# Ending the second batch of a fused top-k attention and MLP kernel the way the first one ends, and re-pacing the layer products around it

## The chip, the core and the metric

One core of a Trainium2 chip runs the whole program. The metric is the device time of one execution in microseconds (us). The kernel before takes 1860.23 us (median of three runs, 1859.75 to 1863.38). The engines are TensorE (PE; PEld is its weight load), VectorE (DVE), ScalarE (ACT), GpSimd (POOL) and SyncE (SP), which issues most of the transfers. Each engine works through its own list of instructions in the order in which the kernel emits them; they meet through semaphores.

## The reference: what is computed

```python
# q, k, v: (8 batches, 8 heads, 576 rows, 64)
scores = matmul(q, k^T) / 8                     # 576 x 576 for each head
kth    = the 32nd largest of each row
scores = where(scores >= kth, scores, -1e9)     # keep the top 32 of a row
attn   = softmax(scores);  o = matmul(attn, v)
x      = o, heads side by side                  # (8, 576, 512)
# then, for each batch, a low-rank mixer over the rows and a two-layer MLP
h = x^T @ U @ V                                 # U: 576 x 32, V: 32 x 576
u = x + h^T
out = u + relu(u @ w1) @ w2                     # w1: 512 x 2048, w2: 2048 x 512
```

Everything is in float32 at the end; the weights U, V, w1, w2 arrive as float64 and the kernel makes float32 of them itself while the first batches run.

The MLP of a batch needs all four head pairs of that batch, since the mixer and both layers work on all 512 columns. So the layer products of batch b can only be computed once the attention of batch b is done. The kernel computes them beside the attention of batch b + 1, and those of the last batch stand alone at the end.

## The kernel before

The work is cut into 160 steps, counted from 0. A step is one block of rows of one head pair: `g, t = divmod(n, 5)`, blocks t = 0 to 3 have 128 rows for each of the two heads (two row chunks of 576 scores), and block t = 4 has the last 64 rows of both heads in one chunk. A batch is 4 pairs, 20 steps. The top 32 of a row are found on VectorE, eight at a time, with four MAX8 and three MATCH_REPLACE8. The weighing of a chunk (exponential on ScalarE, then everything under the 32nd largest set to zero) is spread over three engines:

```python
def front(g, t):
    ...
    for c in order:                              # VectorE: the first eight of each chunk
        nc.vector.max(ms[c], curs[c])            # L320
    yield
    pooled = n == 2 and (g, t) != (NPAIR - 1, NT - 1)
    for i in range(1, TOPK // 8):
        if i == 1:
            nc.scalar.mul(nmax[:, 0:n], first[:, 0:n, 0], -SCALE)
            for c in range(1 if pooled else n):
                weigh(chunks[c], Es[c], nmax[:, c : c + 1])        # L300, ScalarE: exp
        ...                                      # match_replace (L330) and max (L334) by chunk
        yield
    if pooled:                                   # second chunk: mask on GpSimd, exp afterwards
        nc.gpsimd.tensor_scalar(Es[1], chunks[1], ms[1][:, 7:8], NEG, ALU.is_lt, ALU.mult)  # L337
        nc.gpsimd.tensor_tensor(chunks[1], chunks[1], Es[1], ALU.add)                       # L338
    for c in range(1 if pooled else n):          # otherwise: exp first, mask on VectorE
        nc.vector.scalar_tensor_tensor(out=Es[c], in0=chunks[c], scalar=ms[c][:, 7:8],      # L340
                                       in1=Es[c], op0=ALU.is_ge, op1=ALU.mult, accum_out=sums[c])
    ...
    yield
    if pooled:
        weigh(chunks[1], Es[1], nmax[:, 1:2], sums[1])
    yield
```

What follows for a block: `turns` transposes its weights on TensorE and copies them back on ScalarE (three parts, two for t = 4; each part ends in a `yield`), `values` multiplies them with v. When all five blocks of a pair are done, `mixed` transposes the pair's result, scales it by the reciprocals of the row sums (`inverse`, on VectorE; the scaling on GpSimd) and adds the low-rank mixer. After the fourth pair of a batch it puts `mlp(b)`, the layer products, on the list `fillers`:

```python
def inverse(g, lo, hi):
    den = dens[g][:, lo:hi]
    nc.vector.tensor_scalar_add(den, den, 1e-9)  # L378
    nc.vector.reciprocal(den, den)               # L379

def values(g, t):
    ...
    if t == NT:
        inverse(g, 2 * NT if g == NPAIR - 1 else 0, 2 * NT + 1)
    ...

def mixed(g, wait):
    ...                                          # transposes, copy, scaling on GpSimd (L429)
    for _ in range(wait):
        yield
    ...                                          # pT (L435), Tb, up (L447, L449), uT (L457)
    if gi == NPAIR - 1:
        fillers.append(mlp(b))
```

`mlp` yields after each matmul of the first layer (L472) and the second (L491). After each group of four row blocks' columns its result is added to u on GpSimd (L507, on VectorE in the last batch) and turned back by transposes (L519) some matmuls later; the last group is turned back right at the end. One `fill()` places as many layer matmuls as its share allows, and advances the mixing of a pair by one piece:

```python
SLOTS, SHORT, EARLY = 8, 0.65, 0.91
share = MLP_WORK / (NPAIR * SLOTS * (NT + SHORT))

def fill(k=1):
    nonlocal due
    for _ in range(k):
        if mixing and next(mixing[0], True):
            mixing.pop(0)
        due += share * (SHORT if t == NT else 1) * (EARLY if n <= 2 * ALONE + 2 else 1)
        while due > 0:
            if not fillers:
                due = 0.0
                break
            done = next(fillers[0], None)
            ...                                  # due -= done
```

`ALONE` is 20, the number of steps in a batch. The main loop has three forms of a step: one for the first batch (no layer products yet), one for steps 19 and 20, the end of the first batch, and one for all later ones (cut here to the order of its calls):

```python
for n in range(STEPS + 2):
    ...
    if n >= ALONE - 1 and n <= ALONE:            # steps 19 and 20
        list(turning)
        if n < ALONE:
            scores(*divmod(n + 1, CH))
        list(turns(*divmod(n - 1, CH)))
        if n < ALONE:
            values(*divmod(n - 2, CH))
            next(here)                           # step 19's exponential is emitted here
        values(*divmod(n - 1, CH))
        if n < ALONE:
            inverse(g, 0, 2 * NT)
            next(here)
            mixing.append(mixed(g, 1))
            fill(); next(here); next(here)
            continue
        fill(); scores(*divmod(n + 1, CH)); next(here)
        while mixing:
            fill()
        ...
        continue
    if n < ALONE:
        ...                                      # first batch
        continue
    # later batches: values lag by two steps, the mixing of a pair by one more
    fill(); next(turning, None); fill(); next(turning, None); fill(); next(ready, None); fill()
    if n - 2 >= ALONE:
        values(*divmod(n - 2, CH))
    if n + 1 < STEPS:
        scores(*divmod(n + 1, CH))
    next(here, None)                             # the exponential
    ...
    if n - 2 >= ALONE and (n - 2) % CH == NT:
        mixing.append(mixed((n - 2) // CH, 4))
    fill(); next(here, None); fill()
    if n <= STEPS:
        turning = turns(*divmod(n - 1, CH))
    next(turning, None); fill(); next(here, None); next(last, None); ...; fill()
while mixing or fillers:
    fill()
```

Of the kernel before, what the change touches and what calls it, by code (L numbers as in the profile page):

```python
# [24 lines left out]
def kernel(  # L25
# [35 lines left out]
    NT, TAIL = 4, 64  # L61
# [3 lines left out]
    NPAIR = H // 2  # L65
    NP = B * NPAIR
    SCALE = 1.0 / float(D) ** 0.5
    NV = 3
    HT = 10
    PE, ACT = mybir.EngineType.PE, mybir.EngineType.Activation  # L70
# [231 lines left out]
    def front(g, t):  # L302

        if t == 0:
            dens[g] = small.tile([P, 2 * NT + 1], F32, tag="den", name="den", bufs=3)
        chunks, den = S2s.pop((g, t)), dens[g]
        n = len(chunks)
        E2 = attn.tile([P, 2 * S], F32, tag="E", name="E", bufs=3)  # L310
        Es = [E2[:, c * S : (c + 1) * S] for c in range(n)]
        sums = [den[:, 2 * t + c : 2 * t + c + 1] for c in range(n)]
        probs[g, t] = E2
        curs, ms = list(chunks), [None] * n
        first = small.tile([P, 2, 8], F32, tag="first", name="first", bufs=3)
        nmax = small.tile([P, 2], F32, tag="nmax", name="nmax", bufs=4)
        order = (1, 0) if n == 2 else (0,)
        for c in order:
            ms[c] = first[:, c]
            nc.vector.max(ms[c], curs[c])  # L320
        yield
        pooled = n == 2 and (g, t) != (NPAIR - 1, NT - 1)
        for i in range(1, TOPK // 8):
            if i == 1:
                nc.scalar.mul(nmax[:, 0:n], first[:, 0:n, 0], -SCALE)
                for c in range(1 if pooled else n):
                    weigh(chunks[c], Es[c], nmax[:, c : c + 1])
            for c in order:
                nxt = attn.tile([P, S], F32, tag="rr", name="rr", bufs=3)
                nc.vector.match_replace(nxt, ms[c], curs[c], NEG)  # L330
                curs[c] = nxt
            for c in order:
                ms[c] = small.tile([P, 8], F32, tag="m8", name="m8", bufs=8)
# [6 lines that stand above are left out]
            nc.vector.scalar_tensor_tensor(  # L340
                out=Es[c],
                in0=chunks[c],
                scalar=ms[c][:, 7:8],
                in1=Es[c],
                op0=ALU.is_ge,
                op1=ALU.mult,
                accum_out=sums[c],
            )
        if t == NT:
            del qkTs[g]  # L350
# [4 lines that stand above are left out]
# [21 lines left out]
# [7 lines that stand above are left out]
        PT = PTs.pop((g, t))  # L383
        va, vd, vt = (a[g % NV] for a in (vas, vds, vts))
        O = ps_t.tile([P, P], F32, tag="tp", name="O")
        if t == NT:
            den, x = dens[g], xs[g % 2]
            inverse(g, 2 * NT if g == NPAIR - 1 else 0, 2 * NT + 1)
            for j in range(NT + 1):
                nc.tensor.matmul(  # L390
                    O,
                    lhsT=PT[:, j],
                    rhs=va[:, :, j, :] if j < NT else vt,
                    start=(j == 0),
                    stop=(j == NT),
                )
            for h in range(2):
                nc.scalar.mul(x[half(h), NT, half(h)], O[half(h), half(h)], den[half(h), 2 * NT :])
            return
        nc.tensor.matmul(O, lhsT=vd, rhs=PT[:, 2 * NT], start=True, stop=False)  # L400
        for j in range(NT):
            for h in range(2):
                nc.tensor.matmul(  # L403
                    O[half(h)],
                    lhsT=va[:, h, j, :],
                    rhs=PT[:, NT * h + j],
                    start=False,
                    stop=(j == NT - 1),
                )
        if t == 0:  # L410
            XTs[g] = attn.tile([P, MAIN], F32, tag="XT", name="XT")
        nc.scalar.copy(XTs[g][:, cols(t)], O)  # L412
# [124 lines left out]
    CH = NT + 1  # L537
    STEPS = NP * CH
    ALONE = NPAIR * CH


    SLOTS, SHORT, EARLY = 8, 0.65, 0.91
    share = MLP_WORK / (NPAIR * SLOTS * (NT + SHORT))
    fillers, mixing, due = [], [], 0.0

    def fill(k=1):

        nonlocal due
        for _ in range(k):
            if mixing and next(mixing[0], True):  # L550
                mixing.pop(0)
            due += share * (SHORT if t == NT else 1) * (EARLY if n <= 2 * ALONE + 2 else 1)
            while due > 0:
                if not fillers:
                    due = 0.0
                    break
                done = next(fillers[0], None)
                if done is None:
                    fillers.pop(0)
                else:  # L560
                    due -= done

    load(0)
    next_params(1)
    t = 0
# [5 lines left out]
    for n in range(STEPS + 2):  # L571
        g, t = divmod(n, CH)
        if n < STEPS:
            if t == 0 and g + 1 < NP:
                load(g + 1)
            if t == 1 and g + 1 < NP:
                ready = prep(g + 1)
            fronts[n] = front(g, t)
            next(fronts[n])
        here, last = fronts.get(n, iter(())), fronts.pop(n - 1, iter(()))  # L580
        if n >= ALONE - 1 and n <= ALONE:

            list(turning)
            if n < ALONE:
                scores(*divmod(n + 1, CH))
            list(turns(*divmod(n - 1, CH)))
            if n < ALONE:
                values(*divmod(n - 2, CH))
                next(here)
            values(*divmod(n - 1, CH))  # L590
            if n < ALONE:
                inverse(g, 0, 2 * NT)
                next(here)
                mixing.append(mixed(g, 1))
# [9 lines that stand above are left out]
            next_params(1)  # L604
            fill()
            next(last, None)
# [7 lines that stand above are left out]
            next(turning, None)  # L614
            next(turning, None)
            scores(*divmod(n + 1, CH))
            fill()
            if n >= 1:
                turning = turns(*divmod(n - 1, CH))
            if n >= 2:  # L620
                values(*divmod(n - 2, CH))
            next(here)
            next_params(1)
            next(turning, None)
            fill()
            next(last, None)
            next(ready, None)
            next(here)
            fill()
            if n >= 2 and (n - 2) % CH == NT:  # L630
                mixing.append(mixed((n - 2) // CH, 3))
            next(here)
            if t == 1:
                next_params(1)
# [4 lines that stand above are left out]
        next(turning, None)  # L639
        fill()  # L640
        next(turning, None)
        fill()
        next(ready, None)
        fill()
        if n - 2 >= ALONE:
            values(*divmod(n - 2, CH))
        if n + 1 < STEPS:
            scores(*divmod(n + 1, CH))
        next(here, None)
        next_params(1)  # L650
        if n - 2 >= ALONE and (n - 2) % CH == NT:
            mixing.append(mixed((n - 2) // CH, 4))
        fill()
        next(here, None)
# [3 lines that stand above are left out]
        next(turning, None)  # L658
        fill()
        next(here, None)  # L660
        next(last, None)
        if t in (1, 3):
            next_params(1)
        next(here, None)
        fill()
# [33 lines left out]
```

## Time and profile before

| | before |
|---|---|
| time | 1860.23 us |
| TensorE busy | 1750.6 us (94%) |
| its weight loads busy | 1324.0 us (71%) |
| VectorE busy | 1617.2 us (87%) |
| ScalarE busy | 1008.1 us (54%) |
| GpSimd busy | 635.7 us (34%) |
| layer matmuls, both layers (L472, L491) | 557.9 + 562.2 us, 2048 each |
| MAX8 and MATCH_REPLACE8 (L320, L330, L334) | 205.4 + 639.6 + 614.8 us |

The trace counts two matmuls for each float32 matmul of the program that is not a transpose. The span of the profiled execution, 1861.6 us, falls into three parts: the first batch's attention alone (to about 224 us), seven batches in which attention and the layer products of the batch before run side by side (to about 1706 us), and the last batch's products alone (155 us). A share over the whole span mixes these; where the batches matter, the busy times have to be taken stretch by stretch. A busy TensorE in these profiles is modelled from pipelined matmuls and is not a TensorE at its peak.

### The profile page before, as it was taken

To read this page: it belongs to the slowest core of one execution; us is meant where nothing else is said; L and a number is where in the kernel's file an instruction comes from. 1 tells how busy PE (TensorE), PEld (TensorE's weight loads), DVE (VectorE), ACT (ScalarE), POOL (GpSimd) and SP (SyncE) were. 2 spreads that over 40 slices of the span, in tenths; PEclk is the share of its full clock that TensorE was granted. 3 is DMA by queue.
4 is the path that set the end of the run, shared out by engine and by line. 5 is a ranking of instruction groups with operands and counts; after the bars stand their busy time and mean duration, and the time that the engine had idled before them with its cause. 6 is when DMAs were issued, how large, how long until landed. Compare 5 with 4: busy or idle time off the path is not lost.

```text
span 1861.6 us, 29241 instructions
## 1 busy us (share of the span) xinstructions
PE 1750.6 (94%) x10528; PEld 1324.0 (71%) x10528; DVE 1617.2 (87%) x3316; ACT 1008.1 (54%) x2466; POOL 635.7 (34%) x432
## 2 busy tenths in 40 slices
PE   4565789999999999999999999999999999999999
PEld 3443556787777877788777877788777877788677
DVE  7999999999999999999999999999999999996000
ACT  4666677555655555555555555555555555554111
POOL 4556466433333332323233332332323332322000
PEclk7677799999999999999999999999999999999999
DMA  3222222101000010110001010101001010000000
GB/s 98 76 72 75 63 81 81 28 23 32 15 21 22 23 29 21 30 25 24 23 13 31 21 32 20 28 22 27 14 24 27 25 30 21 10 8 7 6 14 12
DMA packets 127296, 58.23 MB, mean 31 GB/s; under 512 B 89904, under 2 KB 124976, under 8 KB 127152
## 3 DMA queue, kind: packets, MB, share of 16 engines
q1 hardware_dynamic: 126096, 56.10, 11.3%
q8 instruction: 84, 1.38, 0.3%
q14 instruction: 60, 0.49, 0.1%
q10 hardware_dynamic: 1056, 0.26, 0.1%
HBM read 46.89 MB, written 9.44 MB: 30 GB/s over the span
## 4 chain that ended last, share of the span: by engine, by line
PE 84%; DVE 10%; ACT 4%; issue 1%; POOL 1%; DMA 0%; POOLq 0%; SPq 0%; DVEq 0%; ACTq 0%
PE mm L472 27%; PE mm L491 26%; PE sc L274 9%; PE O L403 6%; PE tp L367 6%; DVE rr L330 4%; DVE m L334 3%; PE O L390 2%; PE up L447 2%; PE O L400 1%; DVE first L320 1%; PE tp L254 1%; PE tp L519 1%; PE up L449 1%; PE tp L372 1%
## 5 line engine op out<-in xcount | busy, mean ns | idle before, releaser
L334 DVE MAX8 m<-rr 128x8 f32<-128x576 f32 x864 | 614.8, 749 | 5.5
L491 PE MATMUL mm<-hT,w 128*128 128x256 f32 (+1 forms) x2048 | 562.2, 410 | 0.0
L472 PE MATMUL mm<-uT,w 128*128 128x256 f32 (+1 forms) x2048 | 557.9, 411 | 1.5 <-ACT hT L484 1.5
L337 POOL TENSOR_SCALAR E<-Ssb,m 128x576 f32<-128x576 f32 x127 | 285.2, 2246 | 650.7 <-DVE m L334 512.7
L472 PEld LDWEIGHTS mm<-uT,w 128*128 128x128 f32 x2048 | 363.3, 190 | 108.6 <-issue 27.6
L491 PEld LDWEIGHTS mm<-hT,w 128*128 128x128 f32 x2048 | 360.5, 190 | 97.7 <-issue 22.5
L330 DVE MATCH_REPLACE8 rr<-m,rr 128x576 f32<-128x576 f32 x576 | 427.8, 743 | 0.0
L367 PE MATMUL tp<-ident,E 128*128 128x128 f32 x1152 | 184.7, 285 | 53.8 <-ACT E L300 38.7
L368 ACT COPY PT<-tp 128x512 f32<-128x512 f32 x288 | 168.4, 585 | 114.9 <-PE tp L367 113.0
L300 ACT ACTIVATE E<-Ssb,nmax 128x576 f32<-128x576 f32 x288 | 223.8, 778 | 5.9 <-POOL Ssb L338 0.7
L367 PEld LDWEIGHTS tp<-ident,E 128*128 128x128 f32 x1152 | 144.9, 147 | 106.9 <-ACT E L300 50.7
L274 PE MATMUL sc<-qkT 64*128 64x288 f32 (+1 forms) x1280 | 212.5, 454 | 0.3 <-ACT Ssb L293 0.3
L330 DVE MATCH_REPLACE8 rr<-first,Ssb 128x576 f32<-128x576 f32 x288 | 211.8, 742 | 0.0
L320 DVE MAX8 first<-Ssb 128x8 f32<-128x576 f32 x288 | 205.4, 750 | 0.9 <-ACT Ssb L295 0.9
L340 DVE SCALAR_TENSOR_TENSOR E<-Ssb,m,E 128x576 f32<-128x576 f32 x161 | 137.8, 856 | 65.6 <-ACT E L300 48.2
L338 POOL TENSOR_TENSOR Ssb<-Ssb,E 128x576 f32<-128x576 f32 x127 | 178.9, 1408 | 10.6
L484 ACT ACTIVATE hT<-mm 128x320 f32<-128x320 f32 (+1 forms) x256 | 104.4, 408 | 119.8 <-PE mm L472 119.0
L412 ACT COPY XT<-O 128x128 f32<-128x128 f32 x128 | 34.0, 266 | 215.1 <-PE O L403 215.1
L403 PE MATMUL O<-PT,va 128*64 128x128 f32 x2048 | 147.7, 289 | 0.0
L274 PEld LDWEIGHTS sc<-qkT 64*128 64x128 f32 (+1 forms) x1280 | 110.2, 187 | 51.7 <-issue 25.4
L504 DVE TENSOR_TENSOR oT<-uT,mm 128x320 f32<-128x320 f32 (+1 forms) x8 | 3.6, 455 | 146.6 <-PE mm L491 146.6
L403 PEld LDWEIGHTS O<-PT,va 128*64 128x64 f32 x2048 | 116.0, 143 | 16.8 <-issue 2.9
(73 smaller groups left out, 1484.3 us busy)
## 6 DMA issues: line engine op xcount, KB each, us to landing
raw<-in_moe_w_ch_dram SPq DMA_DIRECT2D x32, 512.0 KB, 3.7
va<-in_v_dram SPq DMA_DIRECT2D x64, 128.0 KB, 2.5
out_dram<-ob SPq DMA_DIRECT2D x64, 128.0 KB, 1.9
ld_q<-in_q_dram SPq DMA_DIRECT2D x63, 128.0 KB, 2.8
ld_k<-in_k_dram SPq DMA_DIRECT2D x63, 128.0 KB, 2.8
ld_ends<-in_q_dram SPq DMA_DIRECT2D x32, 32.0 KB, 2.2
ld_ends<-in_k_dram SPq DMA_DIRECT2D x32, 32.0 KB, 2.2
vd<-in_v_dram SPq DMA_DIRECT2D x64, 16.0 KB, 2.0
```

Source lines behind the costliest of these rows:

```text
L274: nc.tensor.matmul(sc[slice(0, n) if t < NT else half(h), h, 0:HALF], lhsT=qkT[half(h), 0, cols(t)], rhs=qkT[half(h), 1, i * HALF : (i + 1 ...
L300: nc.scalar.activation(E, chunk, AF.Exp, bias=nmax, scale=SCALE, accum_out=total)
L320: nc.vector.max(ms[c], curs[c])
L330: nc.vector.match_replace(nxt, ms[c], curs[c], NEG)
L334: nc.vector.max(ms[c], curs[c])
L337: nc.gpsimd.tensor_scalar(Es[1], chunks[1], ms[1][:, 7:8], NEG, ALU.is_lt, ALU.mult)
L338: nc.gpsimd.tensor_tensor(chunks[1], chunks[1], Es[1], ALU.add)
L367: nc.tensor.transpose(tp[:, j, :], E2[:, a : a + P], ident)
L368: nc.scalar.copy(PT[:, NT * h : NT * h + NT], tp)
L403: nc.tensor.matmul(O[half(h)], lhsT=va[:, h, j, :], rhs=PT[:, NT * h + j], start=False, stop=(j == NT - 1),)
L472: nc.tensor.matmul(ph[:, 0:w], lhsT=w1[:, cc, f * P : (f + 1) * P], rhs=uT[:, cc, lo:hi], start=(cc == 0), stop=(cc == NC - 1),)
L491: nc.tensor.matmul(po[:, 0:w], lhsT=w2[:, f, c * P : (c + 1) * P], rhs=hTs[f][:, 0:w], start=(f == 0), stop=(f == NF - 1),)
```

## The change

The second batch gets the ending of the first. In its last step (step 39) the exponential of the short block, the last transposes and both remaining value products are emitted at once rather than trailing into steps 41 and 42, and the mixing of its last pair is done in step 40; the second batch's products can then begin right behind it. Unlike at the first batch, there are products of the batch before to be placed beside this, so the ending calls `fill` between its parts; `fill(False)` places products without advancing the mixing. Step 38's second chunk, too, is weighed without GpSimd, and the reciprocals of the pair's sums are taken in two parts. For the first batch's products to be finished by then, they go faster beside the second batch (pace 1.02 in place of 0.91), and those beside the third go slower (0.91 in place of 1), so that they last until the next ones are ready.

```diff
+    WAITED = (NPAIR - 1, 2 * NPAIR - 1)
...
-        pooled = n == 2 and (g, t) != (NPAIR - 1, NT - 1)
+        pooled = n == 2 and not (g in WAITED and t == NT - 1)
...
-            inverse(g, 2 * NT if g == NPAIR - 1 else 0, 2 * NT + 1)
+            inverse(g, 2 * NT if g in WAITED else 0, 2 * NT + 1)
...
-    SLOTS, SHORT, EARLY = 8, 0.65, 0.91
+    SLOTS, SHORT, PACE = 8, 0.65, {1: 1.02, 2: 0.91}
...
-    def fill(k=1):
+    def fill(mix=True):
         nonlocal due
-        for _ in range(k):
-            if mixing and next(mixing[0], True):
-                mixing.pop(0)
-            due += share * (SHORT if t == NT else 1) * (EARLY if n <= 2 * ALONE + 2 else 1)
+        if mix and mixing and next(mixing[0], True):
+            mixing.pop(0)
+        due += share * (SHORT if t == NT else 1) * PACE.get((n - 1) // ALONE, 1)
...
-        if n >= ALONE - 1 and n <= ALONE:
+        if (n + 1) // CH - 1 in WAITED and t in (NT, 0):
             list(turning)
-            if n < ALONE:
+            fill(t != 0)
+            if t:
                 scores(*divmod(n + 1, CH))
-            list(turns(*divmod(n - 1, CH)))
-            if n < ALONE:
+            for _ in turns(*divmod(n - 1, CH)):
+                fill(t != 0)
+            if t:
                 values(*divmod(n - 2, CH))
                 next(here)
             values(*divmod(n - 1, CH))
-            if n < ALONE:
+            if t:
                 inverse(g, 0, 2 * NT)
                 next(here)
                 mixing.append(mixed(g, 1))
...
-        if n - 2 >= ALONE:
+        behind = n - 2 >= ALONE and n - 1 != 2 * ALONE
+        if behind:
             values(*divmod(n - 2, CH))
...
-        if n - 2 >= ALONE and (n - 2) % CH == NT:
+        if behind and (n - 2) % CH == NT:
             mixing.append(mixed((n - 2) // CH, 4))
```

At the first batch the list of products is still empty, so the new `fill` calls place nothing there.

More of the change, by code (lines that the diff above doesn't have):

```diff
@@ L539 @@
     ALONE = NPAIR * CH
-    SLOTS, SHORT, EARLY = 8, 0.65, 0.91
+    SLOTS, SHORT, PACE = 8, 0.65, {1: 1.02, 2: 0.91}
     share = MLP_WORK / (NPAIR * SLOTS * (NT + SHORT))
     fillers, mixing, due = [], [], 0.0
-    def fill(k=1):
+    def fill(mix=True):
         nonlocal due
-        for _ in range(k):
-            if mixing and next(mixing[0], True):
-                mixing.pop(0)
-            due += share * (SHORT if t == NT else 1) * (EARLY if n <= 2 * ALONE + 2 else 1)
[L553 to L561, printed above, removed]
+        if mix and mixing and next(mixing[0], True):
+            mixing.pop(0)
+        due += share * (SHORT if t == NT else 1) * PACE.get((n - 1) // ALONE, 1)
+        while due > 0:
+            if not fillers:
+                due = 0.0
+                break
+            done = next(fillers[0], None)
+            if done is None:
+                fillers.pop(0)
+            else:
+                due -= done
     load(0)
```

## The prediction

> **What bounds the kernel now.** I number the 160 steps from 0: step n is block t = n mod 5 of head pair g = n div 5, so a batch is 20 steps (4 pairs) and the changed places are steps 38 to 40 (end of the second batch) and the pace of steps 21 to 60. I first read busy time in stretches, cutting at the starts of VectorE's first MAX8 of each pair (timeline of VectorE), one row for each pair of the second batch (223.7 to 434.2 us) and the third (434.2 to 645.8), one for the fourth, one for the end:
>
> ```profile
> core 0: us, PE busy (x) PEld busy (x) DVE busy (x) ACT busy (x) POOL busy (x), PEclk, DMA share, GB/s
> 223.70:276.00 52.30, 48.17 (x273) 32.12 (x271) 51.35 (x110) 39.40 (x88) 32.65 (x22) 1.00 0.26 78
> 276.00:331.60 55.60, 50.52 (x303) 35.47 (x303) 53.44 (x110) 40.26 (x92) 38.19 (x27) 1.00 0.23 68
> 331.60:382.90 51.30, 51.30 (x328) 39.44 (x328) 50.05 (x103) 29.68 (x77) 18.64 (x12) 1.00 0.11 28
> 382.90:434.20 51.30, 51.28 (x338) 41.64 (x337) 50.05 (x103) 29.75 (x75) 16.97 (x11) 1.00 0.09 22
> 434.20:487.80 53.60, 50.02 (x309) 37.72 (x308) 50.08 (x103) 27.83 (x69) 16.88 (x11) 0.97 0.10 25
> 487.80:540.10 52.30, 52.30 (x313) 37.70 (x312) 49.96 (x103) 29.35 (x73) 16.34 (x10) 1.00 0.08 19
> 540.10:593.30 53.20, 53.20 (x330) 39.53 (x330) 49.91 (x103) 29.11 (x76) 18.56 (x12) 1.00 0.11 27
> 593.30:645.80 52.50, 52.50 (x343) 43.16 (x342) 50.00 (x103) 30.13 (x76) 16.20 (x10) 1.00 0.09 22
> 645.80:858.20 212.40, 211.57 (x1318) 161.71 (x1317) 199.86 (x409) 119.00 (x296) 68.76 (x44) 1.00 0.10 24
> 1706.50:1861.60 155.10, 149.74 (x673) 118.27 (x671) 4.24 (x12) 23.64 (x63) 3.21 (x4) 1.00 0.04 12
> ```
>
> Take length minus VectorE's busy time: the two pairs at pace 0.91 that no longer prepare weights (rows 3 and 4) leave VectorE idle 1.25 us each, which is only the small gaps between its instructions. So 51.3 us is VectorE's floor for a pair. At pace 1 the idle time is 3.52, 2.34, 3.29 and 2.50 us (rows 5 to 8), and 12.54 us in the fourth batch. **At 0.91 VectorE sets the time, at 1 TensorE pushes it**: a batch then takes 212.4 us where four floors make 205.2. The last row is the end, 155 us of the last batch's layer products alone.
>
> Second, who ends VectorE's waits in the second batch, in the third, and TensorE's in the third (the waits from 224 to 434 us and from 434 to 646 us: us in total, times, longest; one fence each):
>
> ```profile
> DVE E L340 <- ACT E L300: 2.2, 1, 2.2
> DVE E L340 <- PE tp L367: 1.3, 1, 1.3
> ```
>
> ```profile
> DVE E L340 <- ACT E L300: 7.3, 5, 2.2
> ```
>
> ```profile
> PE tp L519 <- POOL oT L507: 2.9, 1, 2.9
> PE tp L519 <- ACT x L428: 0.7, 1, 0.7
> ```
>
> VectorE's waits are for the exponentials (L300), mostly in the short step t = 4 of a pair, where it has one row chunk (6.7 us) and TensorE more than that. The 2.2 us of the second batch stand at its very beginning, in step 19 (the window opens inside it). TensorE's 2.9 us is a hole at the end of the first batch's products in step 42: the last turning back waits for GpSimd, and the next batch's products stand behind it.
>
> Third, VectorE's timeline at step 19, the end of the first batch that the change copies:
>
> ```profile
> 220.20 0.76 DVE L334 MAX8 m<-rr 128x8 f32<-128x576 f32 x1
> 223.19 0.82 DVE L340 SCALAR_TENSOR_TENSOR E<-Ssb,m,E 128x576 f32<-128x576 f32 x1 [2.23 <-ACT E L300]
> 223.94 0.08 DVE L340 DVE_READ_ACCUMULATOR E<-Ssb,m,E 128x1 f32 x1
> ```
>
> This ending puts the next step's scores, the transposes and one value product of the earlier steps ahead of step 19's exponential; VectorE pays 2.23 us for it.
>
> **What the Trainium skill says.** "Perfetto Trace Analysis", Identifying the Most-Contended Engine, calls matmul busy share a bad measure and prefers weight-load busy share. The trace agrees: TensorE reads 100% busy in row 3 and in row 8, yet its weight loads fill 77% and 82%, and only in the second does VectorE lose time. So I don't take "100%" for "no room". "TensorE: Matmul & The Clock Gate", Architectural detail, has ScalarE and VectorE as strict FIFOs; in step 19 the exponential indeed starts (222.39 us) only after ScalarE has waited 2.63 us for the copy of a value product (L412) ahead of it. "ScalarE: Activation LUTs", What ACT_TABLE_LOAD costs, gives an activation with a pointer bias about 280 ns + 0.833 ns an element, 760 ns for 576 elements; L300's mean is 778 ns. So its own length is no issue, its place in the queue is.
>
> **The change, part by part.**
>
> *Products moved.* The built program's order has 462 of the first batch's 512 layer matmuls (as the trace counts them) ahead of the scores that step 40 issues; the changed one has all 512. From step 63's scores on both orders agree within 2 to 4 matmuls, so the end of the program is the same. In the end stretch 585 such matmuls kept TensorE busy 142.97 us (busy time of this tile), 244 ns each: 50 x 0.244 = **12.2 us of TensorE work move from the third batch to the second**. None is removed.
>
> *Second batch, first two pairs* (rows 1 and 2). By step 31 some 28 of the 50 are placed, 6.8 us. TensorE's idle time there is 52.30 - 48.17 + 55.60 - 50.52 = 9.2 us, so most of it fits beside a VectorE that also prepares weights. I give 0.7 us a pair for the short steps: +1.4.
>
> *Third pair.* Its load becomes that of pace 1, where pairs cost 52.3 to 53.2. I take 53.0 for 51.3: +1.7.
>
> *Fourth pair, with the new ending.* Step 39 costs VectorE a wait like step 19's 2.23. Against it, TensorE's clock is now full (the scores of step 19 took 2.29 us, elsewhere 1.24, and transposes shrink too); for it, 8 layer matmuls now stand between these scores and the value product, 8 x 0.244 = 2.0 us, and TensorE comes in late as in the other pace-1 pairs. I take 3.2 us, against 0.4 of small gaps that this step has today: +2.8. Step 38's second chunk is weighed on VectorE rather than GpSimd: one more L340 of 0.82 us: +0.8. The reciprocals of the 8 finished sums (0.15 + 0.20 us in step 19) come here: +0.35. The fourth pair: about +4.0. **Second batch: +7.1.**
>
> *Third batch.* Its pace becomes 0.91, so each pair should fall to the 51.3 of rows 3 and 4: 53.6 + 52.3 + 53.2 + 52.5 - 4 x 51.3 = 6.4. The 9-column reciprocal pair of step 41 (1.02 + 0.21 us in the timeline) goes, and 0.13 + 0.16 us come: 0.9 less. I keep back 0.4 for leftovers. **Third batch: -6.9.** The 2.9 us hole is inside this: VectorE lost only about 0.8 us to it in step 42.
>
> *Sum*: +7.1 - 6.9 = +0.2 us on 1860.2. I say **1860.0 us**.
>
> **Rivals.**
>
> *TensorE is the bound throughout, and filling its holes is pure gain.* It idles 9.2 us in rows 1 and 2 and 3.6 in row 5. If the end of the attention follows TensorE's total work, filling two thirds of these saves up to 8 us: about 1852. For it: pace 1 exceeds the floor by 7 us a batch. Against: in rows 1 to 4 VectorE has next to no idle time, and cannot finish sooner whatever TensorE does.
>
> *The new ending becomes a wait of its own.* Scores, transposes, two value products, the mixing and the last turning back now stand in one row in steps 39 and 40; if TensorE enters step 39 late, the exponential comes 5 us late instead of 3, and in step 40 TensorE can wait on GpSimd's scaling ahead of the scores for step 41. Against: the first batch's step 20 shows VectorE idle only 0.24 us with the same order, and step 40 is long (10.9 us). That would be about 1865.
>
> *Moving work between two batches that both stand at TensorE's limit is a zero sum.* This is close to my own sum, but for another reason; then the third batch would win about 12 us and the second lose about 12.
>
> **Range and chances.** The sum is a difference of two terms near 7 us, each good to about 3 us: 4 together, some 6 for eight times in ten. So 1854 to 1866. Two per cent is 37 us, three times all that is moved (12.2 us); nothing here reaches it: faster 0.01, same 0.98, slower 0.01.
>
> **What would show it.** In the changed profile the four pairs of the third batch should each be near 51.3 us, with VectorE idle about 1.25 us; the second batch should be near 217 to 218 us instead of 210.5; step 39 should hold a wait of L340's line on L300's of 3 us or so; TensorE's idle time in the first two pairs should fall below 4 us, and the 2.9 us wait on GpSimd should be gone or under 1 us; the fourth batch and the 155 us at the end should be within 1 us of today's. I am wrong if the first two pairs don't grow at all (then it is faster by a few us), if step 39's wait is 5 us or more, if step 40 gains a wait, or if the third batch stays above 208 us.

## The result, and the profile after

The changed kernel takes **1868.33 us** (median of six runs, 1867.48 to 1869.36) against 1859.99 us before (six runs): a ratio of 1.004, 95% interval 1.0027 to 1.0053. It is slower by about 8 us, where 1860.0 us and a range of 1854 to 1866 were predicted.

The same view as in the prediction, busy time in stretches of the changed kernel: the four pairs of the second batch, the four of the third, the fourth batch, the fifth, and the end. In the changed kernel every line number that is cited here is two higher (L302 is the exponential, L342 VectorE's weighing, L509 GpSimd's sum, L521 the turning back).

```profile
core 0: us, PE busy (x) PEld busy (x) DVE busy (x) ACT busy (x) POOL busy (x), PEclk, DMA share, GB/s
221.70:274.00 52.30, 49.06 (x275) 33.07 (x275) 51.28 (x110) 38.22 (x87) 32.65 (x22) 1.00 0.26 78
274.00:333.70 59.70, 54.26 (x320) 38.01 (x319) 52.74 (x110) 40.35 (x93) 38.20 (x27) 1.00 0.22 66
333.70:387.80 54.10, 54.10 (x343) 42.60 (x342) 50.00 (x103) 31.67 (x81) 17.28 (x11) 1.00 0.09 24
387.80:442.30 54.50, 53.95 (x365) 43.87 (x363) 51.89 (x107) 29.83 (x74) 14.83 (x10) 1.00 0.09 23
442.30:492.60 50.30, 49.94 (x294) 36.02 (x293) 49.05 (x103) 29.92 (x74) 16.26 (x10) 1.00 0.10 25
492.60:544.00 51.40, 51.40 (x312) 36.96 (x311) 50.15 (x103) 28.81 (x71) 17.22 (x11) 1.00 0.09 22
544.00:595.30 51.30, 50.45 (x324) 38.60 (x323) 50.05 (x103) 29.71 (x77) 17.18 (x11) 1.00 0.11 29
595.30:646.60 51.30, 50.16 (x332) 41.03 (x331) 50.05 (x103) 29.00 (x72) 16.95 (x11) 1.00 0.09 22
646.60:861.50 214.90, 209.42 (x1291) 158.59 (x1290) 199.71 (x409) 116.53 (x291) 68.11 (x43) 0.98 0.09 23
861.50:1074.40 212.90, 211.86 (x1318) 161.37 (x1317) 199.31 (x409) 118.86 (x297) 69.04 (x44) 1.00 0.09 24
1711.90:1866.50 154.60, 149.23 (x671) 117.89 (x670) 4.30 (x12) 23.19 (x62) 3.21 (x4) 1.00 0.04 12
```

Length before and after, cut in both kernels at the starts of VectorE's first MAX8, says where the time came from:

| | before | after | difference | predicted |
|---|---|---|---|---|
| second batch, pairs 1 and 2 | 107.9 | 111.9 | +4.0 | +1.4 |
| pair 3 | 51.3 | 54.1 | +2.8 | +1.7 |
| pair 4, with the new ending | 51.3 | 54.5 | +3.2 | +4.0 |
| third batch | 211.6 | 204.3 | -7.3 | -6.9 |
| fourth batch | 212.4 | 214.9 | +2.5 | 0 |
| fifth to eighth | 841.5 | 843.7 | +2.2 | 0 |
| the end | 161.6 | 161.0 | -0.6 | 0 |

(The end is counted here from the start of the last step with attention, step 159; the eighth batch stops there.) These rows sum to +6.8 us; the other 1.5 us of the difference between the medians can't be placed from one profile of each kernel. The third batch is at its floor of 51.3 us a pair as foreseen. Most of the excess stands in places that the prediction held to be free or nearly so: the first two pairs, and everything from the fourth batch on. The first batch is left out of the table: its instructions stand in the same order in both, but its last step took 8.9 us in the profiled execution of before and 6.8 us in that of after. In kernels that are identical up to there it varied between 6.8 and 8.9 us from execution to execution, which fits that the median of before lay between 1860.0 and 1861.2 us from one set of runs to the next.

Who ended VectorE's waits in the second batch of the changed kernel, and one of them in its second pair that is not in a short step's usual place (timeline of VectorE):

```profile
DVE E L342 <- ACT E L302: 10.2, 7, 2.9
DVE w L173 <- ACT w L163: 1.0, 1, 1.0
```

```profile
310.63 0.82 DVE L342 SCALAR_TENSOR_TENSOR E<-Ssb,m,E 128x576 f32<-128x576 f32 x1 [2.35 <-ACT E L302]
```

This is a wait for an exponential in step 27, a long step. The 1.0 us in L173 is VectorE's part of preparing a weight, which waits in step 28 for ScalarE's part.

The prediction counted TensorE's idle time in the first two pairs as room. Who ended it, the largest wait and the one for GpSimd, before (223.7 to 331.6 us) and after (221.7 to 333.7):

```profile
PE tp L367 <- ACT E L300: 4.9, 5, 1.8
PE pT L435 <- POOL x L429: 1.1, 1, 1.1
```

```profile
PE tp L369 <- ACT E L302: 3.3, 3, 1.9
PE pT L437 <- POOL x L431: 1.1, 1, 1.1
```

Most of the rest waits for copies and activations on ScalarE.

In the fourth batch TensorE's waits show a hole like the one that the prediction expected to vanish from step 42. It did vanish there. In step 62, where the kernel before waits 0.8 us (first line), the changed kernel waits 3.6:

```profile
PE tp L519 <- POOL oT L507: 0.8, 1, 0.8
```

```profile
PE tp L521 <- POOL oT L509: 3.6, 1, 3.6
PE tp L369 <- ACT x L430: 1.5, 1, 1.5
```

### The profile page after: what moved, and what is told of

The parts are those of the page before. It is cut to its first block, busy times and chain, and to the rows that moved or that the text cites. A ratio compares the mean times of both kernels' runs of the same rounds, so it can differ in the third digit from the quotient of the medians.

```text
span 1866.5 us, 29226 instructions
## 1 busy us (share of the span) xinstructions
PE 1748.1 (94%) x10528; PEld 1318.3 (71%) x10528; DVE 1615.3 (87%) x3320; ACT 1008.0 (54%) x2465; POOL 632.6 (34%) x430
## 3 DMA queue, kind: packets, MB, share of 16 engines
q1 hardware_dynamic: 126096, 56.10, 11.3%
## 4 chain that ended last, share of the span: by engine, by line
PE 81%; DVE 9%; ACT 6%; issue 2%; POOL 2%; DMA 0%; POOLq 0%; DVEq 0%; SPq 0%; ACTq 0%
PE mm L474 25%; PE mm L493 25%; PE sc L276 9%; PE O L405 6%; PE tp L369 6%; DVE rr L332 3%; DVE m L336 3%; PE up L449 2%; PE O L392 2%; ACT E L302 2%; PE O L402 1%; DVE first L322 1%; PE tp L256 1%; PE up L451 1%; PE tp L521 1%
## 5 line engine op out<-in xcount | busy, mean ns | idle before, releaser
L302 ACT ACTIVATE E<-Ssb,nmax 128x576 f32<-128x576 f32 x288 | 223.3, 776 | 6.4 <-POOL Ssb L340 1.2
L342 DVE SCALAR_TENSOR_TENSOR E<-Ssb,m,E 128x576 f32<-128x576 f32 x162 | 135.3, 836 | 71.8 <-ACT E L302 56.4
L405 PE MATMUL O<-PT,va 128*64 128x128 f32 x2048 | 142.8, 282 | 0.0
L405 PEld LDWEIGHTS O<-PT,va 128*64 128x64 f32 x2048 | 111.7, 139 | 16.2 <-issue 1.6
```

What stands on the lines that cost most here:

```text
L302: nc.scalar.activation(E, chunk, AF.Exp, bias=nmax, scale=SCALE, accum_out=total)
L405: nc.tensor.matmul(O[half(h)], lhsT=va[:, h, j, :], rhs=PT[:, NT * h + j], start=False, stop=(j == NT - 1),)
```

## The experiments

My theory after reading the traces had four parts: the higher pace costs more beside the preparation of weights than I allowed (A, D); the new ending costs little; a hole has moved to the fourth batch (C); and something small repeats in every later batch. The rivals: the ending is the cost (B), the hole only shows that TensorE has nothing to do, and the later batches carry a lag along.

### The ending alone, and the pace alone

`end_only` is the changed kernel with the old pace:

```diff
-        due += share * (SHORT if t == NT else 1) * PACE.get((n - 1) // ALONE, 1)
+        due += share * (SHORT if t == NT else 1) * (0.91 if n <= 2 * ALONE + 2 else 1)
```

> The changed kernel with the old pace (0.91 up to step 42, then 1): the new ending alone; from step 43 on the products stand as in the kernel before. Theory A (the higher pace beside the second batch costs the time, the ending little): steps 38 to 41 together +1 to +3 us (one more 0.82 us weighing on VectorE, a wait of 1 to 2 us in step 39, one reciprocal pair less), the first three pairs of the second batch unchanged, 1861 to 1863 us. Theory B (the ending costs it: its products, transposes and value products ahead of step 39's exponential): steps 38 to 41 +5 us or more, about 1866 us.

Measured: 1860.64 us, 1.000 of before (0.9991 to 1.0009). Steps 38 to 41 together took 0.02 us less than in the kernel before (+0.73, +0.14, +0.25, -1.14): the extra weighing on VectorE is paid back by the reciprocal pair that step 41 no longer has. That is less than the +1 to +3 us of theory A, and theory B falls. Step 39 did not wait at all here (idle 0.41 us, the usual gaps).

`pace_only` is the kernel before with the higher pace in the second batch and 1 after it:

```diff
-            due += share * (SHORT if t == NT else 1) * (EARLY if n <= 2 * ALONE + 2 else 1)
+            due += share * (SHORT if t == NT else 1) * (1.02 if ALONE < n <= 2 * ALONE else 1)
```

> The kernel before with pace 1.02 in steps 21 to 40 and 1 from there: the old ending, so TensorE runs out of products in step 40 and has none until step 42. Theory A: the second batch's first three pairs grow by 7 us together, as in the changed kernel (+4.0 and +2.8 in its second and third), and the third batch, at pace 1, stays near 211 us: 1866 to 1868 us. Theory B: the second batch grows by 2 us at most, about 1861 us.

Measured: 1870.20 us, 1.0051 of before (1.0036 to 1.0066). The second batch grew by 9.1 us, the pairs by 1.3, 3.2, 2.8 and 1.8; steps 27 to 29 and 34 are nearly those of the changed kernel (12.7, 12.4, 10.1 and 8.9 us). The third batch shrank by 3.5 us, more than expected: it has fewer products (444 matmuls of the trace, not 491), and its step 42 has no hole any more; no run separates the two. Batches four to eight took 0.5 us more each here too, and the total is above the 1866 to 1868 us of theory A. Its core holds: **the pace costs the time; the ending, in this kernel with its hole, nothing.** (Without the hole it does cost something, see `end_late`.)

### The hole at the end of a batch's products

`after_late` and `before_late` let the last group of a batch be turned back within the next batch's products, like every other group, in the changed kernel and in the kernel before:

```diff
+    late = []
     def mlp(b):
         uT = uTs.pop(b)
-        late = []
...
-        late.pop()()
+        if b == B - 1:
+            late.pop()()
```

> The changed kernel with the last group of a batch turned back in the next batch's products (after its fourth relu), like every other group, in place of right at the end; only the last batch's stays. Theory C (the 3.6 us hole in step 62, where TensorE's transposes wait for GpSimd's sum behind the 3.6 us masking of a chunk, costs the fourth batch 2.5 us): step 62 falls from 13.75 to about 11 us and the like steps of later batches (82, 102 and so on) by 0.8 each, 1862 us. Rival (the hole only shows that TensorE has nothing to do): no more than 1 us, 1867.5 us.

Measured: 1856.71 us, 0.9979 of before (0.9972 to 0.9987), 11.6 us below the changed kernel, where theory C gave it about 6. TensorE's wait for GpSimd's sum is gone from the fourth batch; the longest wait left there (the view shown above for TensorE, now of `after_late`):

```profile
PE tp L369 <- ACT x L430: 1.5, 1, 1.5
```

Step 62 fell from 13.75 to 10.87 us, and step 64, two steps on, from 8.75 to 6.66. The fourth batch fell by 6.1 us, each later one by 1.06.

> The kernel before with the same edit. Theory C: step 42 loses 0.7 us of VectorE's wait, steps 62, 82 and so on 0.9 each, together 5 to 6 us: 1854 to 1855 us. Rival: within 1 us of 1860.

Measured: 1849.77 us, 0.9943 of before (0.9928 to 0.9957): 11.3 us less by the medians, twice what theory C gave it. The third batch fell from 211.6 to 206.9 us although its hole was 2.9 us and VectorE lost only 0.7 us in the step itself. The stretches of `before_late`, third and fourth batch:

```profile
431.90:638.90 207.00, 206.31 (x1292) 157.21 (x1291) 200.39 (x409) 116.08 (x290) 67.44 (x43) 1.00 0.10 24
638.90:850.20 211.30, 211.30 (x1319) 161.68 (x1318) 199.82 (x409) 118.77 (x296) 68.77 (x44) 1.00 0.10 24
```

TensorE went from 208.0 busy of 211.6 us in the third batch to 206.3 of 207.0, and the short steps 44, 49 and 54 took 1.6, 1.1 and 1.7 us less: the hole had reached VectorE, by way of a TensorE that stayed late, over three pairs. The rival (no more than 1 us) falls. Why the hole exists is in GpSimd's timeline of the changed kernel around step 62: the last sum stands behind the masking of a chunk.

```profile
668.34 2.21 POOL L339 TENSOR_SCALAR E<-Ssb,m 128x576 f32<-128x576 f32 x1 [3.43 <-PE tp L369]
670.63 1.40 POOL L340 TENSOR_TENSOR Ssb<-Ssb,E 128x576 f32<-128x576 f32 x1
671.99 0.73 POOL L509 TENSOR_TENSOR oT<-oT,uT 128x256 f32<-128x256 f32 x1
```

In the changed kernel the products that pace 0.91 leaves for steps 61 and 62 run out earlier in step 62 than they did before (20 and 12 matmuls of the trace in these steps, against 33 and 20), so TensorE arrives at these transposes with less work ahead of it and waits 3.6 us in place of 0.8. `pace_only` fits this: its third batch goes at pace 1, its steps 61 and 62 have 33 and 19 matmuls, and the wait is 0.8 us.

### Preparing the weights before the products begin

`after_prep` is the changed kernel with two pieces of weight preparation in each step of the first batch but the short ones; until now only the steps with t = 1 had a second one:

```diff
             next(here)
-            if t == 1:
+            if t < NT:
                 next_params(1)
```

> The changed kernel with all weights prepared in the first batch: one more piece of preparation in every step of it but the short one, none left for steps 20 to 30 (VectorE's share of it, some 11 x 0.41 us, moves along, from one batch to the other). Theory D (the first two pairs of the second batch can't take more products because three activations of weight preparation, 2.1 us, stand ahead of a pair's scaling and of the exponential in ScalarE's queue): the waits of steps 27 to 29, now 2.4, 1.1 and 3.2 us, fall to the usual 0.2 and 1.7 in step 29; these two pairs together about 5 us less beyond the 4.5 us that move to the first batch, 1864 us. Theory E (it is the amount of products alone, wherever they stand): these steps keep waits of 4 us together beyond the gaps, 1868 us.

Measured: 1860.07 us, 0.9992 of before (0.9984 to 1.0001), 8.3 us below the changed kernel, more than expected. The first two pairs of the second batch in stretches:

```profile
222.50:273.60 51.10, 49.86 (x277) 35.20 (x277) 49.85 (x105) 30.58 (x73) 20.84 (x13) 0.97 0.08 18
273.60:326.10 52.50, 52.42 (x316) 37.87 (x317) 50.05 (x103) 27.27 (x69) 17.22 (x11) 1.00 0.10 25
```

VectorE's idle time in the second pair is 52.50 - 50.05 = 2.45 us, against 59.70 - 52.74 = 6.96 in the changed kernel; steps 27, 28 and 29 waste 0.2, 0.2 and 1.6 us in place of 2.4, 1.1 and 3.2. The first batch grew by only 1.1 us by taking the preparation over. Theory E falls: the same products at the same pace (222 matmuls of the trace in these two pairs, in both) cost these waits only beside the preparation. ScalarE's timeline of the changed kernel shows one way in which they meet, in step 26:

```profile
295.96 0.67 ACT L163 ACTIVATE w<-raw 128x512 f32<-128x512 f32 x1
296.54 0.76 ACT L165 ACTIVATE raw<-raw,four 128x512 f32<-128x512 uint8 x1
297.20 0.76 ACT L166 ACTIVATE raw<-raw,nudge 128x512 f32<-128x512 f32 x1
297.86 0.56 ACT L430 COPY x<-tp 128x512 f32<-128x512 f32 x1
```

The copy of a pair's result stands behind three activations of preparation; the scaling on GpSimd follows it, and TensorE waits 1.1 us for that with its list standing still. The run removes the preparation on all engines at once, ScalarE's three activations, VectorE's one and GpSimd's two operations, so it doesn't tell which of them weighs most.

`before_late_prep` has the same edit on top of `before_late`.

> The kernel before with the last group turned back in the next batch's products and all weights prepared in the first batch. If preparation beside products costs waits even at pace 0.91 (step 29 waits 1.6 us today): 1 to 2 us less than without the early preparation, 1848 us. If the first batch pays more for it (its ScalarE and GpSimd are busier then): 1850 us or more.

Measured: 1846.15 us, 0.9918 of before (0.9903 to 0.9933), 3.6 us below `before_late`, also more than expected. The second batch falls from 210.4 to 205.0 us, its floor, and the first one grows by 1.1. So preparation beside products cost waits even at pace 0.91. This run also tells what the added products cost where no weights are prepared: its second batch's first two pairs take 102.4 us at pace 0.91 (209 matmuls), those of `after_prep` 103.6 at 1.02 (222). That is +1.2 us, against +4.0 beside the preparation.

### The remainder of the shares

`after_phase` is the changed kernel with the running remainder set to the value that it has in the kernel before:

```diff
     for n in range(STEPS + 2):
         g, t = divmod(n, CH)
+        if n == 3 * ALONE + 3:
+            due = -0.5968
```

> The changed kernel with the remainder of the shares set in step 63 to the value that it has in the kernel before (-0.597), so that from the scores of step 65 on TensorE's list is the same as before; today single matmuls stand one slot earlier or later. If the 0.54 us that batches five to eight each lost come from this rounding: 2 to 2.5 us less, 1866 us, and these batches at 212.4 us. If they come from something carried over (TensorE's lag): unchanged, 1868.3 us.

Measured: 1865.46 us, 1.0023 of before (1.0015 to 1.0031), 2.9 us below the changed kernel. Batches five to seven are at 212.37 us, as before the change, and step 64 of the fourth lost 1.2 us. So the half microsecond of each later batch came from single matmuls that stand a slot earlier or later, and not from a lag that is carried along. The fourth batch fell by 1.8 us although TensorE still waits 3.6 us in step 62.

### Putting the parts together

`end_late` is `after_late` at the old pace (the edit of `end_only`).

> The changed kernel's ending at the old pace (0.91 up to step 42, then 1), with the last group turned back in the next batch's products. The ending alone changed nothing (1860.6 to 1861.1 us) and the late turning back gave 11.3 us without it. If the two add up: 1849.5 us. If the ending also helped to fill the hole that is now gone: 1851 us.

Measured: 1852.30 us, 0.9951 of before (0.9936 to 0.9966), 2.5 us above `before_late`. The ending alone no longer comes for nothing once the hole is gone: it places 18 matmuls of the trace fewer in the second batch (440 for 458) and the third batch, at pace 1, pays 1.9 us for them, mostly in steps 49 and 54. The second theory comes nearer: in `end_only` the new ending had also shortened TensorE's idle time in step 42, from 2.9 to 1.3 us.

`after_all` is the changed kernel with all three edits: late turning back, early preparation, and the remainder set.

> The changed kernel with the late turning back, the weights prepared in the first batch and the remainder set in step 63: the change with its three side costs taken away. If the parts add up, 1868.3 - 11.6 - 8.3 - 2.9 = 1845.5 us, about 0.6 under the kernel before with the same late turning back and early preparation (1846.15): the change in itself is worth nothing. If new ending and pace have a gain of their own once nothing hides it (TensorE fuller in the second batch), 1843 us or less.

Measured: 1845.59 us, 0.9922 of before (0.9907 to 0.9937). The parts add up: 1868.3 - 11.6 - 8.3 - 2.9 = 1845.5. Against `before_late_prep` (1846.15 us) that is no difference that these runs resolve. What the second, third and fourth batch take in the two, `after_all` first:

```profile
223.60:436.80 213.20, 211.35 (x1297) 160.21 (x1297) 201.82 (x415) 119.26 (x294) 68.96 (x44) 0.98 0.09 22
436.80:641.10 204.30, 201.81 (x1257) 152.54 (x1256) 199.31 (x409) 117.37 (x293) 67.63 (x43) 1.00 0.10 24
641.10:848.80 207.70, 205.84 (x1288) 156.71 (x1287) 199.06 (x409) 116.14 (x290) 68.04 (x43) 1.00 0.09 24
```

```profile
222.70:427.70 205.00, 199.77 (x1233) 149.88 (x1234) 200.01 (x411) 117.41 (x292) 72.38 (x46) 0.99 0.09 23
427.70:634.70 207.00, 206.32 (x1292) 157.16 (x1291) 200.38 (x409) 116.23 (x290) 67.52 (x43) 1.00 0.10 24
634.70:846.00 211.30, 211.30 (x1319) 161.63 (x1318) 199.97 (x409) 118.92 (x296) 68.85 (x44) 1.00 0.10 24
```

The sums are 625.2 and 623.3 us; the profiled execution of `after_all` was the slowest of its four (1848.3 us), and the second pair of its second batch took 53.6 us where `after_prep`, the same program up to there, took 52.5. Batch by batch the change costs +8.2, -2.7 and -3.6 us here. It moves work between the second batch and the next two, and what these gain the second about pays. Both versions beat the kernel before by some 14 us.

`best_short` was to use this: `before_late_prep` with a smaller share for the short steps, where VectorE's waits stand.

```diff
-    SLOTS, SHORT, EARLY = 8, 0.65, 0.91
+    SLOTS, SHORT, EARLY = 8, 0.45, 0.91
```

> The kernel before with late turning back, early preparation and a share of 0.45 in place of 0.65 for the short step of a pair (the others take 4 per cent more). VectorE's remaining waits stand in the short steps, where it works 6.7 us. If the products placed in these steps are what delays their exponentials: steps 64, 69, 74, 79 wait about 0.4 us less each and it takes 11 us less over the seven batches at most, 1836 to 1843 us. If TensorE is simply behind by the whole pair's load, the wait moves but stays: 1846 us.

Measured: 1857.78 us, 0.9985 of before (0.9979 to 0.9992), 11.6 us above `before_late_prep`, which neither side expected. The waits moved as the second theory has it, and grew: the fourth batch takes 213.4 us for 211.3, with a new wait of 1.2 us in step 72 and the like, and the short steps 74 and 79 still waste 2.2 us each. How the shares lie within a pair is as fine a balance as their sum; I leave open why 0.65 suits it.

## Why the prediction was wrong

What held is that work moved from one batch to another gains next to nothing: in `after_all`, with the side costs taken away, the change comes out at 0.6 us under its counterpart, which can't be told from the predicted +0.2 or from zero. That the sum agrees there is in part luck, since its terms are others (+8.2, -2.7, -3.6 us where +7.1, -6.9 and 0 were predicted). Two terms of the real change agree in number and not in cause. The third batch came to its floor (-7.3 us for -6.9), but `before_late` gets 4.7 of this at the old pace, by removing the hole that the prediction had at 0.8. The fourth pair cost +3.2 for +4.0, but the ending alone (`end_only`) costs this pair 0.9 us, the pace alone (`pace_only`) 1.8. The result left the range through terms that the sum had too small or lacked:

- **The first two pairs, +1.4 predicted, +4.0 measured.** The failed step is "TensorE's idle time there is ... 9.2 us, so most of it fits". That idle time was not room. It was TensorE waiting in order, mostly for ScalarE and 1.1 us for GpSimd, which had weights to prepare; in the changed kernel it is still 8.7 us (52.30 - 49.06 + 59.70 - 54.26), though TensorE is busy 4.6 us longer. (The 28 products by step 31, 6.8 us, were nearly right in number, 30 in the trace; but these two pairs are steps 20 to 29 and got only 20 of them.) `after_prep` removed the cause: the waits of steps 27 to 29 fall to the usual ones, 1.3 us of idle TensorE are left in the two pairs, and the added products cost them 1.2 us, near the predicted 1.4.
- **The fourth batch, 0 predicted, +2.5 measured.** I read from the orders of both programs that they agree from step 63 on, and took equal order for equal time. But the hole stands in step 62, ahead of that, and depends on how far TensorE is behind when it arrives at the transposes, and pace 0.91 had brought it there early. Step 62 alone takes 2.0 us more than before (13.75 for 11.75). The +2.5 is a net figure all the same: `after_late`, which removes the hole, takes 6.1 us off this batch, and `after_phase`, which leaves it and moves single matmuls, 1.8 us, 1.2 of it in step 64. How much of the +2.5 belongs to each stays open. My own view of step 42 had shown the wait and its releaser.
- **The later batches, 0 predicted, +2.2 measured.** That both orders "agree within 2 to 4 matmuls, so the end of the program is the same" is the same mistake once more: `after_phase` shows that these matmuls are the whole of it, 0.54 us a batch.
- **The third pair, +1.7 predicted, +2.8 measured.** The term was mis-sized; 54.1 us is above what any pair of the third batch took before. VectorE waits 2.3 us more in its short step 34, and `after_prep` leaves that as it is (2.67 us idle in both), so the preparation is not its cause; what makes it more than a pair at pace 1 stays open.
- **Step 39's wait, about 3 us predicted, 1.50 measured**, and none in `end_only`. The term was put too high; the rival that the ending becomes a wait of its own was wrong.

I also wrote that the 2.9 us hole of step 42 cost VectorE only about 0.8 us. That is what VectorE loses in that step. `before_late` shows 4.7 us over the batch, most of it in the short steps of the next three pairs.

The prediction's reading of weight-load shares doesn't hold either. In its own table row 4 fills 81% with weight loads and VectorE loses nothing, while row 6 fills 72% and VectorE loses 1.1 us over the gaps. Rows 3 and 8, which it compared, happen to fit; the share doesn't tell a free pair from a loaded one here.

## What to carry to other kernels

Before moving work into an engine's idle time, ask what ends that idle time: if it waits in order for another engine, the work added may not fill the gap but come on top of it (here 4.6 us of work made two pairs 4.0 us longer). A wait in the list of a nearly full engine can be paid by its consumers several steps later (here 0.7 us in the step itself and 4.7 over the batch), so its cost is to be read from the following steps too. Giving a late consumer's work (here the last turning back of a batch) some independent work ahead of it was worth 11 us, more than any re-pacing tried here.

## What the runs showed that I had not expected

- A hole of 2.9 us in TensorE's list, removed, saved 4.7 us in its batch; holes of 0.8 us saved 1.05 us in each later batch. The edit left all arithmetic as it was.
- Moving single matmuls by one slot, a pattern that repeats in each batch, was worth 0.54 us of 212.4 us a batch.
- In programs that are the same up to there, the length of step 19 varied from 6.8 to 8.9 us between executions, while TensorE's granted clock over the first batch stayed under full (0.67 to 0.78 in stretches of 50 us of before, up to 200 us). No run shows whether the one causes the other.
